# Attention and a gated feed-forward in one program: merged score visits, a planner with transfer times by kind, and 136 small matmuls on constants at the start

## The chip, the cores and the metric

The kernel runs on one core of one Trainium2 chip. The metric is the device time of one execution in microseconds. Engines: TensorE (PE; its weight loads are PEld), VectorE (DVE), ScalarE (ACT), GpSimd (POOL), and SyncE (SP), which here issues every DMA.

## The reference

Causal attention over 4 batches, 12 heads, 448 tokens and 64 numbers per head, then a gated feed-forward on 1792 tokens:

```python
scores = scale * np.matmul(q, k.transpose(0, 1, 3, 2))
scores = np.where(mask, -1000000000.0, scores)
attn = np.exp(scores - np.max(scores, axis=-1, keepdims=True))
attn = attn / (np.sum(attn, axis=-1, keepdims=True) + 1e-09)
x = np.matmul(attn, v)          # then heads side by side: 1792 x 768
a = x @ w1
b = x @ w2
h = a * b @ w3
return h @ w_out
...
```

w1 and w2 are 768x1024, w3 1024x1024, w_out 1024x768. The weights arrive as 64-bit floats, q, k and v as 32-bit floats.

## The kernel before

**The work.** Weights are decoded to f32 on chip: two ScalarE passes (lines 681, 683), a shift on VectorE (685) and an integer add on VectorE or GpSimd (688). Since h is only multiplied by w3 and then w_out, the product W3W_out is made once (`w34`: transposes of w3 on line 768, f32 products on 780). For every batch, six pairs of heads give values x (`pair`), then the gate products x w1 and x w2 (`gate`, lines 904 to 906), then the projection by W3W_out (`project`, 964 to 966). f16 operands are split into a high and a low half, so each product is three matmuls.

**A pair of heads.** q and k are turned on TensorE (batches 0 and 1, line 492) or by DMA (batches 2 and 3). Scores (line 575) use half of the array's rows per head for three blocks of query rows (128x128, 128x256, 128x384 of scores) and a quarter of the array for the last 64 rows (64x448). VectorE adds the mask and takes the maximum (592), ScalarE the exponential (596). The result is scaled and split (621 to 628), transposed by DMA, and multiplied with the values (648, 653), where half of the array's columns serve each head. So TensorE's array has four shapes: whole, row halves, quarters, column halves; the planner calls them `mode`.

**What sets the order.** Every step is put into `Program` with a due time, its possible engines with a cost for each, and what it reads and writes. `order()` then runs a list schedule: at each time the ready step of the lowest due time goes on the engine that is free first. This plans PSUM banks, engines and the DMA queue, and the instructions are emitted in that order; at run time each engine goes through its list in order and waits where it must. Due times come from the numbers in `PLAN`. Before, a transfer costs its size over one rate (181 or 330 GB/s) and the queue is free again after a fixed time. A planned change of mode costs `SWITCH`.

**The places that the change touches:** `PLAN` (27), `add` (64), `order` (90), the constants (292), `dma` (440), `scores` (565), its calls in `pair` (635), `raw` (695), `take_w3` (745).

Of the kernel before, what the change touches and what calls it, by code (L numbers as in the profile page):

```python
# [26 lines left out]
PLAN = dict(nc=10, wstep=3.6064, soft=-6.8718, w0=50.8305, w34=0.7706, ab=1.9504, out=0.6632, gap=-1.6322, lat=44.2335, begin=-91.0074, wlead=70.5419, urgent=-469.9817, flex=370.3401, sc=-41.0893, vo=-494.4237, av=-194.2706, x=-353.7633, qlead=-514.025, rlead=417.269, v0=250.3178, v1=137.6978, gram=2, nf=3, h0=0, hv=1, ns=7, wo0=372.2276, wo1=301.1492, wom=91.9573, w3a=767.9653, w3l=46.2422, wd=-104.1576, wh=-132.8946, wl=1.1959, fin=-10.7242, ev=483.517, po=[7.835, -22.3194, -46.2642, -45.7187, -46.1544, -168.5123, 44.732, 118.2718, -2.1469, -154.505, -36.8352, 4.8443, 45.9944, -62.3407, -59.3789, -141.4965, -13.9926, -146.366, -84.3586, -180.0751, 32.2385, 37.7583, 62.9194, 45.468], wo=[94.042, -8.263, -88.9315, -217.7217, 115.6771, 99.8526, 211.7957, -24.8481], w3=[-158.8005, -50.8167, -61.9442, -32.663, -51.9857, -143.9432, 16.037, 208.3012], tw=[-214.4914, 58.2404, 21.4694, -22.4979, -112.6908, -172.2348, -114.743, -134.9378, -53.1451, -19.9257, -4.9187, -20.2346, -61.9799, -199.5703, -107.2525, -134.2498], slack=0.1918, pflex=136.6935, fq=2, hlead=80.6809, stick=24.2514, wfrom=6)  # L27
# [10 lines left out]
WINDOW, PHASE = 3.413, 1.65  # L38

# [11 lines left out]
class Program:  # L51
# [3 lines left out]
    def __init__(self):  # L55
        self.ops, self.writer, self.readers, self.modes = [], {}, {}, {}
        self.port, self.lock = set(), set()
        self.banks, self.leased, self.first = {}, [], {}
# [5 lines left out]
    def add(self, due, how, reads=(), writes=(), stage=None, mode=None, port=False, lock=False):  # L64
# [18 lines left out]
        if mode:  # L83
            self.modes[i] = mode
        if port:
            self.port.add(i)
# [11 lines left out]
    def order(self):  # L98
# [11 lines left out]
        ran = [None] * n  # L110
        dma_free, last_mode, lock_end, port_end = 0.0, None, 0.0, 0.0
# [28 lines left out]
        while len(result) < n:  # L140
# [41 lines left out]
            if e == SP:  # L182
                move, turn = cost
                dma_free = max(dma_free, t + (1.275 if turn else 1.1)) + move
                free[e] = max(t + 0.65, dma_free - 0.93) if turn else t + 0.475
                end = dma_free + 0.91
            else:
# [9 lines left out]
                if e == PE and cost:  # L197
                    mode = self.modes.get(i)
                    if mode != last_mode:
                        cost += SWITCH  # L200
                        last_mode = mode
                    end = matmul(t, cost)
# [40 lines left out]
def tile_causal_attention_moe(ctx: ExitStack, tc: tile.TileContext, q, k, v, w1, w2, w3, wo, out):  # L243
    nc = tc.nc
# [47 lines left out]
    nc.vector.memset(ones, 1.0)  # L292
    mask = cst.tile([P, 3 * P], BF16, name="mask")
# [146 lines left out]
    def dma(dst, src, due, reads, writes, size, turn=False, rate=330e3):  # L440
        kw = {"transpose": True} if turn else {}
        prog.add(due, (SP, (size / (181e3 if turn else rate), turn),
# [15 lines left out]
    def take_v(b, half, due):  # L458
# [7 lines left out]
        for c in range(4):  # L466
            rows = min(P, S - c * P)
            dma(t[0:rows, c], v[b, heads, c * P : c * P + rows].rearrange("h p d -> p h d"), due - 6, (), [vk[c]],
                NP * rows * D * 4, rate=181e3)
# [11 lines left out]
    def turned_whole(p, b, hs, T, qk, qkk, qt, qtk):  # L481

        for i, src in ((1, k), (0, q)):
            dma(qk[0:QP, i], src[b, hs].rearrange("h (p r) d -> p r h d", r=4),
                T - PLAN["qlead"], (), [qkk + (i,)], 2 * S * D * 4, rate=181e3)
# [15 lines left out]
    def halved(p, b, hs, T, qk, qkk, qt, qtk):  # L501
# [4 lines left out]
        for i, src in ((1, k), (0, q)):  # L506
            raw_k = [qkk + (i, n) for n in range(3)]
            for h in range(2):
                dma(qk[:, i, 0:3, h], src[b, hs.start + h, 0 : 3 * P].rearrange("(c p) d -> p c d", p=P), T - PLAN["qlead"],
                    [], [raw_k[h]], 3 * P * D * 4, rate=181e3)  # L510
            dma(qk[0:D, i, 3], src[b, hs, 3 * P : S].rearrange("h p d -> p h d"), T - PLAN["qlead"],
                [], [raw_k[2]], 2 * D * D * 4, rate=181e3)
# [23 lines left out]
    def pair(p):  # L536
# [28 lines left out]
        def scores(us, due):  # L565
            i, c, w, lo = place(us[0])
            n = min(P, S - c * P)
            banks = [prog.lease("sc") for _ in us]
            m = mask_t if i == 2 else mask[:, (2 - c) * P :]

            def products(qs, ks, start, stop):
                for j in range(2):
                    rows = slice(j * D, (j + 1) * D)
                    ps = banks[j if i < 2 else 0][0]
                    nc.tensor.matmul(ps[rows if i == 2 else slice(0, P), :w], qs[rows, c * P : c * P + n], ks[rows, 0:w],  # L575
                                     start=start, stop=stop)

            def both():
                if not halves:
                    products(qt[:, 0], qt[:, 1], True, True)  # L580
                    return
                q16 = qt.rearrange("p i f -> p (i f)").bitcast(F16).rearrange("p (i t f) -> p i t f", i=2, t=2)
                for m_, (a, b_) in enumerate(((0, 0), (0, 1), (1, 0))):
                    products(q16[:, 0, a], q16[:, 1, b_], m_ == 0, m_ == 2)

            outs = [heads[place(u)[0]] for u in us]
            prog.add(due, (PE, (3 if halves else 4) * t_mm(w) + 0.02, both), [qtk + (1,), qtk + (0,)],
                     [key for _, key in banks] + [tk + (c,) for _, tk in outs] + ([tk for _, tk in outs] if p < 2 else []),
                     mode="quad" if i == 2 else "row")
            for u, (ps, key), (t32, tk) in zip(us, banks, outs):  # L590
                o = t32[:, lo : lo + w]
                prog.add(due + 0.4, (DVE, t_dve(w) + 0.07, lambda o=o, ps=ps, u=u: nc.vector.tensor_tensor_reduce(  # L592
# [472 lines left out]
```

## Time and profile before

| | |
|---|---|
| median of 3 runs | 555.8 us (554.55 to 556.99) |
| profiled execution | 555.84 us |
| span of the profile | 554.0 us |
| TensorE busy | 537.5 us, 97% of the span |
| VectorE busy | 384.4 us, 69% |
| ScalarE busy | 323.9 us, 58% |
| GpSimd busy | 156.1 us, 28% |
| moved by DMA | 84.60 MB, mean 153 GB/s |

Busy is the time in which at least one instruction of the engine was running. Matmuls overlap one another, so a row's duration is longer than the distance to the next row's start; the distance is what one of them costs TensorE. An f32 product of line 780 shows as two records.

### The profile page before, as it was taken

What the parts mean: (1) busy time and instruction counts of PE and PEld (TensorE: products, weight loads), DVE (VectorE), ACT (ScalarE), POOL (GpSimd) and SP (SyncE); (2) the same over time, 40 slices, a digit from 0 to 9 for tenths busy, and PEclk for the clock granted to TensorE, in tenths of its full rate; (3) what the DMA queues carried; (4) which work ended last, traced back from release to release, by engine and by line L of the source; (5) the groups of instructions that cost most, each with busy time, mean ns of one, the idle gap of its engine ahead of it and who ended that gap; (6) DMA issues with size and microseconds to landing.
All of it is one profiled execution on the core that took longest, in us unless ns stands there. A gap on an engine that the chain in (4) does not pass through costs nothing.

```text
span 554.0 us, 10756 instructions
## 1 busy us (share of the span) xinstructions
PE 537.5 (97%) x3872; PEld 300.5 (54%) x3872; DVE 384.4 (69%) x1057; ACT 323.9 (58%) x774; POOL 156.1 (28%) x118
## 2 busy tenths in 40 slices
PE   2999999999999999999999999999999999999996
PEld 1565565555554555555445555655555555555564
DVE  5536999998999899984998768398986760322100
ACT  6757888798698978654664646265762551111111
POOL 4000465554566424430334203231421110000000
PEclk9999999999999999999999999999999999999999
DMA  8998599989989648998777958979899235000011
GB/s 324 289 298 233 118 217 206 229 215 240 184 216 239 153 97 151 180 178 167 107 155 142 166 128 167 185 164 159 142 142 143 61 84 115 0 2 1 14 58 43
DMA packets 224950, 84.60 MB, mean 153 GB/s; under 512 B 205952, under 2 KB 221824, under 8 KB 224896
## 3 DMA queue, kind: packets, MB, share of 16 engines
q1 hardware_dynamic: 224896, 83.91, 72.1%
q8 instruction: 30, 0.49, 0.4%
q14 instruction: 24, 0.20, 0.1%
HBM read 43.78 MB, written 5.51 MB: 89 GB/s over the span
## 4 chain that ended last, share of the span: by engine, by line
PE 82%; DVE 9%; ACT 3%; DMA 3%; issue 1%; POOL 1%; POOLq 0%; ACTq 0%
PE sc L575 8%; PE mm L780 8%; PE mm L904 7%; PE mm L905 7%; PE mm L906 7%; PE mm L964 5%; PE mm L966 4%; PE mm L965 4%; PE tr L904 4%; PE av L653 4%; PE tr L905 4%; PE tr L906 4%; PE sc L780 2%; PE tr L964 2%; PE tr L966 2%; PE tr L965 2%
## 5 line engine op out<-in xcount | busy, mean ns | idle before, releaser
L906 PE MATMUL mm<-xt,w 128*128 128x448 f16 x258 | 90.9, 352 | 1.3 <-DVE w L727 1.3
L904 PE MATMUL mm<-xt,w 128*128 128x448 f16 x258 | 91.1, 353 | 0.0
L905 PE MATMUL mm<-xt,w 128*128 128x448 f16 x258 | 90.9, 352 | 0.0
L596 ACT ACTIVATE p<-p,mx 128x384 f32<-128x384 f32 (+2 forms) x144 | 71.5, 497 | 28.7 <-DVE mx L592 28.6
L780 PE MATMUL mm<-wof,w3t 128*128 128x384 f32 x192 | 71.4, 505 | 2.5 <-POOL wof L688 2.5
L628 DVE SCALAR_TENSOR_TENSOR ph<-p,rc,ph 128x384 f16<-128x384 f32 (+2 forms) x144 | 68.6, 528 | 1.4 <-ACT ph L623 0.9
L625 POOL TENSOR_SCALAR ph<-p,rc 128x128 f16<-128x128 f32 (+2 forms) x40 | 43.1, 1086 | 69.8 <-DVE rc L606 39.5
L575 PE MATMUL sc<-qkt 64*128 64x384 f16 (+7 forms) x480 | 58.9, 356 | 0.2 <-DMA qkt<-da 0.2
L906 PEld LDWEIGHTS <-w 128*128 128x128 f16 x384 | 37.5, 98 | 37.1 <-DVE w L727 2.2
L904 PEld LDWEIGHTS <-w 128*128 128x128 f16 x384 | 37.5, 98 | 36.0 <-issue 3.5
L905 PEld LDWEIGHTS <-w 128*128 128x128 f16 x384 | 37.5, 98 | 29.7 <-issue 0.2
L964 PE MATMUL mm<-w34h,arena 128*128 128x384 f16 x152 | 49.7, 327 | 0.0
L966 PE MATMUL mm<-w34h,arena 128*128 128x384 f16 x152 | 49.5, 326 | 0.0
L965 PE MATMUL mm<-w34l,arena 128*128 128x384 f16 x152 | 49.5, 326 | 0.0
L780 PEld LDWEIGHTS mm<-wof,w3t 128*128 128x128 f32 x192 | 34.2, 193 | 24.3 <-issue 4.1
L904 PE MATMUL tr<-xt,w 128*128 128x448 f16 x126 | 44.5, 353 | 0.0
L905 PE MATMUL tr<-xt,w 128*128 128x448 f16 x126 | 44.4, 352 | 0.0
L906 PE MATMUL tr<-xt,w 128*128 128x448 f16 x126 | 44.4, 352 | 0.0
L592 DVE CUSTOM_DVE_ANT_0 p<-sc,mask,qiv 128x384 f32<-128x384 f32 (+2 forms) x72 | 31.4, 478 | 18.0 <-PE sc L575 17.8
L930 ACT CAST arena<-g 128x448 f16<-128x448 f32 x22 | 12.4, 563 | 49.2 <-DVE g L925 49.2
L623 ACT ACTIVATE ph<-p,rc 128x384 f16<-128x384 f32 (+2 forms) x64 | 29.1, 504 | 9.5 <-issue 5.7
L685 DVE TENSOR_SCALAR da<-da 128x768 int32<-128x768 int32 (+1 forms) x38 | 24.2, 639 | 14.9 <-ACT da L681 14.7
(182 smaller groups left out, 1028.8 us busy)
## 6 DMA issues: line engine op xcount, KB each, us to landing
arena<-in_moe_w_dram SPq DMA_DIRECT2D x11, 768.0 KB, 5.7
vr<-in_v_dram SPq DMA_DIRECT2D x24, 192.0 KB, 3.9
out_dram<-osb SPq DMA_DIRECT2D x24, 192.0 KB, 2.2
arena<-in_moe_w_dram SPq DMA_DIRECT2D x8, 512.0 KB, 5.1
xt<-in_moe_w_dram SPq DMA_DIRECT2D x5, 768.0 KB, 8.0
qkr<-in_k_dram SPq DMA_DIRECT2D x12, 224.0 KB, 6.3
qkr<-in_q_dram SPq DMA_DIRECT2D x12, 224.0 KB, 6.9
arena<-in_moe_w_out_dram SPq DMA_DIRECT2D x3, 768.0 KB, 9.3
```

The costliest lines, as they stand in the source:

```text
L575: nc.tensor.matmul(ps[rows if i == 2 else slice(0, P), :w], qs[rows, c * P : c * P + n], ks[rows, 0:w], start=start, stop=stop)
L592: prog.add(due + 0.4, (DVE, t_dve(w) + 0.07, lambda o=o, ps=ps, u=u: nc.vector.tensor_tensor_reduce(out=o, in0=ps[:, :w], in1=m, scale=iv, ...
L596: prog.add(due + 0.9, (ACT, t_act(w, pointers=1, acc=True), lambda o=o, u=u: nc.scalar.activation(out=o, in_=o, func=AF.Exp, scale=-1.0, b ...
L625: (POOL, 1.1 * (t_pool(w) + 0.35e-3 * w + 0.16), lambda src=src, r=r, h=h: nc.gpsimd.tensor_scalar(out=h, in0=src, scalar1=r, scalar2=None ...
L628: prog.add(due + 0.4, (DVE, t_dve(w) + 0.06, lambda src=src, r=r, h=h, l=l: nc.vector.scalar_tensor_tensor(out=l, in0=src, scalar=r, in1=h ...
L780: prog.add(due, (PE, 4 * t_mm(NH), lambda: nc.tensor.matmul(ps[:, :NH], w3t[slot(m)][:, g], wof[:, g, ns], start=g == 0, stop=g == KF - 1) ...
L904: nc.tensor.matmul(ps[:, :S], w[:, 0, d], xh, start=d == 0, stop=False)
L905: nc.tensor.matmul(ps[:, :S], w[:, 0, d], xl, start=False, stop=False)
L906: nc.tensor.matmul(ps[:, :S], w[:, 1, d], xh, start=False, stop=d == KD - 1)
L964: nc.tensor.matmul(t, gh[:, fc, cs], w34h[:, fc, ns], start=fc == 0, stop=False)
L965: nc.tensor.matmul(t, gh[:, fc, cs], w34l[:, fc, ns], start=False, stop=False)
L966: nc.tensor.matmul(t, gl[:, fc, cs], w34h[:, fc, ns], start=False, stop=fc == KF - 1)
```

## The change

The scores of the second and the first block of a pair go into one step: their results lie side by side in the same PSUM bank (columns 0 to 255 and 256 to 383), TensorE makes them in one visit, and a pair leases five score banks instead of seven; the quarters may use bank `tr` too. The planner gets the transfer's rate by kind (164 to 430 GB/s), a count of its packets with a limit on those under way, engines that begin at different times, and a due time for each half of a w3 row; all numbers of `PLAN` are new. 34 steps without inputs, of four 128-column products of a constant each (136 matmuls), stand last in line for TensorE, so `order()` puts them where nothing else is ready.

```diff
-PLAN = dict(nc=10, wstep=3.6064, soft=-6.8718, ...
+PLAN = dict(nc=10, wstep=6.9304, soft=-564.0239, ... join=0, nwarm=34, w3h=[-138.4231, ...
+BEGIN = {PE: 1.3, ACT: 2.1, DVE: 0.85, POOL: 1.3, SP: 0.5}
+RING = 2150
...
-        free = {e: 0.0 for e in (PE, ACT, DVE, POOL, SP)}
+        free = dict(BEGIN)
...
-                move, turn = cost
-                dma_free = max(dma_free, t + (1.275 if turn else 1.1)) + move
-                free[e] = max(t + 0.65, dma_free - 0.93) if turn else t + 0.475
+                move, turn, count = cost
+                begun = max(dma_free, t + (1.07 if turn else 1.22))
+                dma_free = begun + move
                 end = dma_free + 0.91
+                if turn:
+                    free[e] = max(t + 0.65, dma_free - 0.6 - 0.5 * move)
+                else:
+                    free[e] = t + (0.6 if count > 800 else 0.43)
+                    total = count
+                    for a, b, m in reversed(moves):
+                        if b <= free[e]:
+                            break
+                        if total + m > RING:
+                            free[e] = max(free[e], b - (b - a) * (RING - total) / m)
+                            break
+                        total += m
+                    moves.append((begun, dma_free, count))
...
+    def idle_work():
+        ps, key = prog.lease("tr", "mm", "sc")
+
+        def products():
+            for i in range(4):
+                nc.tensor.matmul(ps[:, i * P : (i + 1) * P], ones, ones, start=True, stop=True)
+
+        prog.add(1e6, (PE, 4 * t_mm(P), products), (), [key])
+
+    for _ in range(PLAN["nwarm"]):
+        idle_work()
...
-        def scores(us, due):
-            i, c, w, lo = place(us[0])
-            n = min(P, S - c * P)
-            banks = [prog.lease("sc") for _ in us]
+        def scores(groups, due):
+
+            blocks = []
+            for us in groups:
+                i, c, w, lo = place(us[0])
+                if c == 0:
+                    shared, at = blocks[-1][1], blocks[-1][2] + blocks[-1][4][2]
+                else:
+                    shared, at = [prog.lease("sc") if i < 2 else prog.lease("sc", "tr") for _ in us], 0
...
-        for n, us in enumerate(((2, 5), (1, 4), (6,), (0, 3))):
-            scores(us, T + PLAN["sc"] + 0.6 * n)
+        for n, groups in enumerate(([[(2, 5)], [(1, 4), (0, 3)], [(6,)]], [[(2, 5), (6,)], [(1, 4), (0, 3)]])[PLAN["join"]]):
+            scores(groups, T + PLAN["sc"] + 0.6 * n)
...
             for h in range(2):
+                d = due + h + (PLAN["w3h"][m] if h else 0.0)
                 ns = slice(h * n, (h + 1) * n)
-                t, tk = raw(words(w3[m * P : (m + 1) * P, ns]), n, due + h - PLAN["rlead"])
-                decode(t, tk, n, due + h, w3p[:, ns], [("w3s", h)])
+                t, tk = raw(words(w3[m * P : (m + 1) * P, ns]), n, d - PLAN["rlead"])
+                decode(t, tk, n, d, w3p[:, ns], [("w3s", h)])
```

**The order that comes of it.** First TensorE at its start. Before, transposes of w3 (`tr`) and the first products of w_out with a transposed w3 (`mm`, `sc`) follow one another:

```order
L768 MATMUL tr_70<-ident,arena 128x128 x8
L780 MATMUL mm_64<-wof,w3t_122 128x384
L780 MATMUL mm_65<-wof,w3t_122 128x384
L768 MATMUL tr_70<-ident,arena 128x128 x4
L780 MATMUL sc_66<-wof,w3t_123 128x384
```

Now (136 small matmuls on `ones`, of which the first and the last of each group are shown):

```order
L318 LDWEIGHTS ones
L318 MATMUL mm_64<-ones 128x128
...
L814 MATMUL tr_70<-ident,arena 128x128 x4
L318 LDWEIGHTS ones
L318 MATMUL sc_67<-ones 128x128
...
L826 MATMUL mm_64<-wof,w3t_122 128x384
L826 MATMUL mm_65<-wof,w3t_122 128x384
L826 MATMUL mm_64<-wof,w3t_122 128x384
L826 MATMUL mm_65<-wof,w3t_122 128x384
L814 MATMUL tr_70<-ident,arena 128x128 x4
L523 MATMUL sc_66<-ident,qkr_82 128x112 x4
```

Before the first product now stand 72 small matmuls, four transposes, 52 small ones, four transposes and 12 small ones; then four products of the first two blocks of w_out, and the turns of k and q earlier than before.

SyncE's first transfers, before (in_moe_w_dram is w3 here; the w_out block, `xt`, is third):

```order
L443 DMA arena<-in_moe_w_dram 128x1024 x2
L443 DMA xt_101<-in_moe_w_out_dram 128x1536
L443 DMA w34h<-in_moe_w_dram 128x1024
L443 DMA w34l<-in_moe_w_dram 128x1024
L443 DMA w34h<-in_moe_w_out_dram 128x1536
```

and now:

```order
L474 DMA w34l<-in_moe_w_dram 128x1024
L474 DMA arena<-in_moe_w_dram 128x1024
L474 DMA xt_101<-in_moe_w_out_dram 128x1536
L474 DMA w34h<-in_moe_w_out_dram 128x1536
L474 DMA w34h<-in_moe_w_dram 128x1024
L474 DMA w34l<-in_moe_w_dram 128x1024
L474 DMA qkr_82<-in_k_dram 112x8x64
L474 DMA qkr_82<-in_q_dram 112x8x64
```

(one more w3 piece into `arena` stands ahead of both lists' second row). Two blocks of w_out come after three pieces of w3, and k and q of the first pair right behind seven transfers.

Third, the score products of the first pair on TensorE (`qkt_84`). Before:

```order
L575 MATMUL sc_69<-qkt_84 128x384
L575 MATMUL sc_66<-qkt_84 128x384
L407 LDWEIGHTS ones
L407 MATMUL sc_67<-w34m_126,ones 128x1
L780 MATMUL sc_68<-wof,w3t_124 128x384
L780 MATMUL mm_64<-wof,w3t_122 128x384 x2
L575 MATMUL sc_69<-qkt_84 128x256
L575 MATMUL sc_66<-qkt_84 128x256
L780 MATMUL mm_64<-wof,w3t_122 128x384
L768 MATMUL tr_70<-ident,arena 128x128 x4
```

Now:

```order
L826 MATMUL sc_66<-wof,w3t_124 128x384
L826 MATMUL av_63<-wof,w3t_124 128x384
L613 MATMUL sc_67<-qkt_84 128x256
L613 MATMUL sc_68<-qkt_84 128x256
L613 MATMUL sc_67<-qkt_84 128x128
L613 MATMUL sc_68<-qkt_84 128x128
L523 MATMUL sc_69<-ident,qkr_82 128x112 x4
```

The 256-wide and the 128-wide block are one visit, with no whole-array work between them. Over the whole program TensorE's list changes the shape of the array 168 times before and 130 times now; f32 products of line 780 (now 826) stand right behind scores, values or a small bf16 product 21 times before and 16 times now.

## Rows read from the trace of the kernel before

**Rows 1.** Busy time by stretch; columns: length, PE, PEld, DVE, ACT, POOL, clock, DMA share, GB/s.

```profile
0.00:50.00 50.00, 39.45 (x144) 23.44 (x144) 23.91 (x42) 33.15 (x51) 6.86 (x15) 1.00 1.07 303
50.00:150.00 100.00, 98.97 (x646) 56.76 (x648) 94.01 (x249) 82.26 (x198) 52.17 (x32) 1.00 0.93 195
150.00:250.00 100.00, 99.56 (x776) 55.64 (x771) 94.77 (x267) 79.92 (x187) 45.79 (x30) 1.00 0.86 176
250.00:350.00 100.00, 99.78 (x851) 54.06 (x850) 78.42 (x236) 57.66 (x160) 26.73 (x23) 1.00 0.79 146
350.00:450.00 100.00, 100.00 (x845) 54.66 (x845) 73.38 (x218) 51.73 (x145) 22.83 (x18) 1.00 0.78 142
```

**Rows 2.** Timeline of TensorE's start: start us, us, engine, instruction, [idle before <-releaser].

```profile
6.67 1.08 PE L768 MATMUL tr<-ident,arena 128*128 128x128 f32 x4 [6.67 <-DVE arena L688]
12.01 2.93 PE L780 MATMUL mm<-wof,w3t 128*128 128x384 f32 x4 [2.46 <-POOL wof L688]
14.73 1.06 PE L768 MATMUL tr<-ident,arena 128*128 128x128 f32 x4
16.96 1.46 PE L780 MATMUL sc<-wof,w3t 128*128 128x384 f32 x4
```

**Rows 3.** Busy time by stretch, the first 20 us.

```profile
0.00:10.00 10.00, 2.20 (x8) 1.43 (x8) 4.02 (x12) 5.96 (x9) 2.45 (x12) 1.00 0.79 286
10.00:20.00 10.00, 7.31 (x22) 4.39 (x23) 8.05 (x11) 8.64 (x14) 3.13 (x2) 1.00 1.09 371
```

**Rows 4.** Timeline, the last matmul.

```profile
549.46 0.33 PE L966 MATMUL mm<-w34h,arena 128*128 128x384 f16 x1
```

**Rows 5.** Timeline of TensorE, from gate products to scores.

```profile
255.03 0.35 PE L905 MATMUL tr<-xt,w 128*128 128x448 f16 x1
255.21 0.35 PE L906 MATMUL tr<-xt,w 128*128 128x448 f16 x1
255.50 0.66 PE L575 MATMUL sc<-qkt 64*128 64x384 f16 x6
```

**Rows 6.** Timeline of TensorE: f32 products in a run, and after scores.

```profile
25.09 0.81 PE L780 MATMUL sc<-wof,w3t 128*128 128x384 f32 x2
25.74 0.81 PE L780 MATMUL av<-wof,w3t 128*128 128x384 f32 x2
...
53.54 0.91 PE L780 MATMUL mm<-wof,w3t 128*128 128x384 f32 x2
54.29 0.60 PE L768 MATMUL tr<-ident,arena 128*128 128x128 f32 x4
54.72 0.49 PE L780 MATMUL mm<-wof,w3t 128*128 128x384 f32 x1
```

**Rows 7.** Timeline of TensorE: three places where it waited.

```profile
141.38 0.36 PE L906 MATMUL mm<-xt,w 128*128 128x448 f16 x1 [1.03 <-DVE w L727]
...
179.21 0.36 PE L906 MATMUL mm<-xt,w 128*128 128x448 f16 x1 [0.27 <-DVE w L727]
...
272.78 0.97 PE L575 MATMUL sc<-qkt 64*128 64x384 f16 x11 [0.22 <-DMA qkt<-da]
```

**Rows 8.** Timeline of TensorE: products with a weight load each, and what follows.

```profile
153.31 1.42 PE L855 MATMUL sc<-xt 128*128 128x128 f16 x23
154.66 0.20 PE L407 MATMUL sc<-vam,ones 128*128 128x1 bf16 x2
```

**Rows 9.** Timeline of ScalarE and VectorE: decoding one block of w_out.

```profile
8.28 0.91 ACT L681 ACTIVATE da<-xt 128x768 f32<-128x768 f32 x1
...
14.90 0.96 DVE L688 CUSTOM_DVE_ANT_0 wof<-w34h,da 128x1536 uint16<-128x1536 uint16 x1
```

**Rows 10.** Groups by form: xcount | busy us, mean ns of one | idle before.

```profile
L722 DVE TENSOR_SCALAR w<-da,w_s 128x768 f16<-128x768 f32 x4 | 3.9, 979 | 0.1
L628 DVE SCALAR_TENSOR_TENSOR ph<-p,rc,ph 128x384 f16<-128x384 f32 x48 | 31.1, 650 | 0.4 <-POOL ph L625 0.4
...
L855 PEld LDWEIGHTS <-xt 128*128 128x128 f16 x72 | 4.3, 98 | 0.7
```

More of the change, by code (lines that the diff above doesn't have):

```diff
@@ L484, in turned_whole @@
             dma(qk[0:QP, i], src[b, hs].rearrange("h (p r) d -> p r h d", r=4),
[L485 removed]
+                T - PLAN["qlead"], (), [qkk + (i,)], 2 * S * D * 4, rate=172e3, count=2 * S)
         for i in (1, 0):
@@ L574, in products @@
                     ps = banks[j if i < 2 else 0][0]
-                    nc.tensor.matmul(ps[rows if i == 2 else slice(0, P), :w], qs[rows, c * P : c * P + n], ks[rows, 0:w],
+                    nc.tensor.matmul(ps[rows if i == 2 else slice(0, P), at : at + w], qs[rows, c * P : c * P + n], ks[rows, 0:w],
                                      start=start, stop=stop)
             def both():
-                if not halves:
-                    products(qt[:, 0], qt[:, 1], True, True)
-                    return
@@ L582, in both @@
[L582 to L589, printed above, removed]
@@ L590, in scores @@
-            for u, (ps, key), (t32, tk) in zip(us, banks, outs):
-                o = t32[:, lo : lo + w]
-                prog.add(due + 0.4, (DVE, t_dve(w) + 0.07, lambda o=o, ps=ps, u=u: nc.vector.tensor_tensor_reduce(
-                    out=o, in0=ps[:, :w], in1=m, scale=iv, scalar=-NEG,
-                    op0=ALU.add, op1=ALU.min, accum_out=mx[:, u : u + 1])),
-                    [key, ivk, "mask_t" if i == 2 else "mask"], [mk + (u,), tk + (c,)] + ([tk] if p < 2 else []))
-                prog.add(due + 0.9, (ACT, t_act(w, pointers=1, acc=True), lambda o=o, u=u: nc.scalar.activation(
-                    out=o, in_=o, func=AF.Exp, scale=-1.0, bias=mx[:, u : u + 1], accum_out=sm[:, u : u + 1])),
-                    [mk + (u,)], [tk + (c,), smk + (u,)])
+                for block in blocks:
+                    if not halves:
+                        products(block, qt[:, 0], qt[:, 1], True, True)
+                        continue
+                    q16 = qt.rearrange("p i f -> p (i f)").bitcast(F16).rearrange("p (i t f) -> p i t f", i=2, t=2)
+                    for m_, (a, b_) in enumerate(((0, 0), (0, 1), (1, 0))):
+                        products(block, q16[:, 0, a], q16[:, 1, b_], m_ == 0, m_ == 2)
@@ new lines, in scores @@
+            keys = {id(l): l for b_ in blocks for _, l in b_[1]}
+            outs = [(heads[place(u)[0]][1], b_[4][1]) for b_ in blocks for u in b_[0]]
+            mode = ["quad" if b_[4][0] == 2 else "row" for b_ in blocks]
+            cost = sum((3 if halves else 4) * t_mm(b_[4][2]) + 0.02 for b_ in blocks) + SWITCH * (mode[0] != mode[-1])
+            prog.add(due, (PE, cost, both), [qtk + (1,), qtk + (0,)],
+                     list(keys.values()) + [tk + (c,) for tk, c in outs] + ([tk for tk, _ in outs] if p < 2 else []),
+                     mode=mode[0], leave=mode[-1])
@@ new lines, in scores @@
+            for us, banks, at, m, (i, c, w, lo) in blocks:
+                for u, (ps, key) in zip(us, banks):
+                    t32, tk = heads[place(u)[0]]
+                    o = t32[:, lo : lo + w]
+                    prog.add(due + 0.4, (DVE, t_dve(w) + 0.07, lambda o=o, ps=ps, u=u, at=at, w=w, m=m: nc.vector.tensor_tensor_reduce(
+                        out=o, in0=ps[:, at : at + w], in1=m, scale=iv, scalar=-NEG,
+                        op0=ALU.add, op1=ALU.min, accum_out=mx[:, u : u + 1])),
+                        [key, ivk, "mask_t" if i == 2 else "mask"], [mk + (u,), tk + (c,)] + ([tk] if p < 2 else []))
+                    prog.add(due + 0.9, (ACT, t_act(w, pointers=1, acc=True), lambda o=o, u=u: nc.scalar.activation(
+                        out=o, in_=o, func=AF.Exp, scale=-1.0, bias=mx[:, u : u + 1], accum_out=sm[:, u : u + 1])),
+                        [mk + (u,)], [tk + (c,), smk + (u,)])
```

34 lines of the change are left out of this document (21 added, 13 removed).

## The prediction

> **What bounds the kernel now.** I read the stretches first, because they show which engine is full and when. TensorE is busy 98.97 to 100.00 of every 100 us from 50 us to 450 us; only the first 50 us have a hole, 39.45 busy of 50 [rows 1]. The other engines have room over the whole span, but VectorE (DVE) is at 94.01 and 94.77 of 100 in the two stretches from 50 to 250 us [rows 1]: it is the second bound. A busy TensorE need not be a productive one, so the next view is the start of its timeline, and then the distance from one instruction's start to the next's. The profiled execution took 555.84 us with a span of 554.0; the median of the runs is 555.8, so a sum made against the one holds for the other.
>
> The start shows two losses. TensorE does nothing until 6.67 us, when the first piece of w3 is decoded, and waits 2.46 us before its first product at 12.01 [rows 2]. And it is slow: four product records (two products) take 2.93 us at 12.01 and 1.46 at 16.96 [rows 2]. The granted clock reads 1.00 in both ten-microsecond stretches [rows 3], but twice the time for the same form is the lower level, 1.2 GHz, against 2.4 later. The transposes at 14.73 are still slow, the row at 16.96 is at full pace [rows 2]: the engine had then worked for some 4.5 us since 12.01, with no hole as long as a microsecond.
>
> From 16.96 us to the last matmul, which ends at 549.8 [rows 2, 4], TensorE is a queue without holes. A row of the gate products follows its neighbour by 0.18 to 0.19 us (255.03, 255.21), but the row that changes the shape of the array (whole array to the 64-row halves of the scores) comes 0.29 later [rows 5]: a change of shape costs 0.09 to 0.10 us. A second small price: two f32 records just after scores take 0.75 us to the next start (53.54 to 54.29), two in the middle of a run 0.65 (25.09 to 25.74) [rows 6]; 0.10 per return. True waits are few: 1.03 us at 141.38 and 0.27 at 179.21 for a weight that VectorE makes, 0.22 at 272.78 for a transfer [rows 7]; 1.5 us, and the rest is smaller.
>
> **The change part by part.** *The start.* The rows after the change put 136 small matmuls ahead of the first real products: 72, four transposes, 52, four transposes, 12. Their operand is ready at about 1 us. They cost time only if they last longer than the data take. 23 products, most of 128 columns and each with its own weights, take from 153.31 to 154.66 [rows 8], 0.059 us on the mean; at half pace 0.118. If the pace doubles after 4.5 us of work, as it did between 12.01 and 16.96 [rows 2], 38 run slowly until 5.6, the other 34 of the first group until 7.6, transposes until 8.1 (0.44 for four, from 54.29 to 54.72 [rows 6]; the row reads 0.60 there and 1.06 at 14.73), 52 until 11.1, transposes until 11.6, 12 until 12.3.
>
> When are the data there? The transfers come in the new order: three w3 pieces of 0.52 MB, two w_out blocks of 0.79, two w3 pieces, k, q. 2.86 MB had moved by 10 us, then 371 GB/s went on [rows 3]. The first block (2.36 MB in all) lands at about 8.9, the second (3.15) at 10.8, the next w3 pieces at 12.2 and 13.6, k at 14.2, q at 14.8. A block needs two ScalarE passes of 0.91 and one VectorE join of 0.96 [rows 9], 2.8: ready at about 11.7 and 13.6. So the first product stands ready at 11.7 and the small matmuls let it go at 12.3; two products take 1.3, the next two start at 13.6 anyhow and end at 14.9. Transposes and k, q turns follow as their data come, to 16.8. By then real work of 16 transposes (1.75), four products (2.6) and eight turns (about 0.75) is done, 5.1 us at full pace, and by 16.96 5.25. The kernel before had by 16.96 done 16 transposes and two products, 3.05. **Gain 2.2 us**, at most 3.1 (no hole between 11.7 and 16.8), and at worst a loss (rival 2).
>
> *Fewer changes of shape.* In the order, rows of TensorE change their shape 168 times before and 130 times after: scores of two blocks share a bank and a visit, and the planner keeps a shape longer. 38 x 0.093 (0.29 less the usual distance [rows 5]) makes **3.5 us less**, since the path runs over TensorE wherever that falls; 24 of the 38 lie between the start of the second and the third batch's gate products, after 250 us, where VectorE is at 78 of 100 [rows 1]. Returns to f32 products right after other work fall from 21 to 16: 5 x 0.10, **0.5 us less**. The products themselves are the same in number and shape.
>
> *Waits.* The new plan is made with transfer times by kind instead of one rate, but the trace cannot show its waits. Bounds: none (1.5 us less) and, if each of 24 pairs met its transfer as late as the one at 272.78 did, 24 x 0.22, 5.3 us more. I take **no change**, since the order in hand was also a plan and came out with these 1.5 us in 533; that row is nearer than either end.
>
> *What hides the rest.* 136 matmuls are not on the path while data are missing; if they outlast the data, all of them are. VectorE takes work over from GpSimd: up to the last value of the second batch its order has five joins and three weight scalings more (0.96 and 0.98 us for 768 columns [rows 9, 10]; two joins have 512) and a few small ones, less five copies of attention values, about 5 us; its idle time hides them (rival 1 if not). The tail after 549.8 (4.2 us of scaling and output) [rows 4] is the same.
>
> Sum: 555.84 - 2.2 - 3.5 - 0.5 = **549.6 us**.
>
> A rule against the start's gain is the Trainium skill's, in "TensorE: Matmul & The Clock Gate", section "Back-to-back issue gap": in a stream of weight loads and matmuls one of 128 columns takes about 81 ns, not the isolated gap. The measurement here, 59 ns with the weights loaded each time [rows 8], speaks against it. By 81 ns the small matmuls would end at about 14.4 instead of 12.3, and the sum, by an estimate from that page, would be 551.6; with the loads as the limit this is the milder form of rival 2 below.
>
> **The rivals.**
>
> *1. VectorE becomes the bound (slower).* For: it idles only 11.2 us between 50 and 250 [rows 1], and up to the second batch's last value its order holds about 11 us more work than before: some 5 as above, the rest softmax work of one more pair pulled ahead (seven remainders, 0.65 for the widest common one [rows 10], and four score passes, about 6). TensorE arrives earlier by 2.2 + 0.5 + 12 x 0.093, 3.8. Against: before the first scale of a finished W3W_out row the new order has about 7 us more of this work (14 instructions at some 0.5: qk copies, score passes, decodes), in the first 50 us, where VectorE was busy 23.91 of 50 [rows 1]. That leaves 11 - 7 = 4 to find, and 11.2 - 4 - 3.8 = 3.4 us idle: enough if it can be used. If VectorE keeps all of its 11.2 idle (waits for others), the stretch is 7.8 longer than planned, 557.4; if the early part is not used either, 14.8, 564.4. I price it at 560. It decides if VectorE still idles over about 6 us there.
>
> *2. The small matmuls stay at the low pace.* Then 136 x 0.118 = 16.0, two groups of transposes at 0.87, and the first product starts at 18.9 with 0.9 of real work done, where before about 5.0 was (3.05 at 16.96): 4.1 lost, and 4.5 us more at half pace, 2.2. With the later 4.0 gained: 555.84 + 4.1 + 2.2 - 4.0 = 558.1. For: nothing shows that products on constants bring the pace up. Against: the start [rows 2], where transposes and products did. A milder form: their weight loads, 0.098 us each [rows 10], do not hide behind them and set the distance. Then the same chain ends at 16.1 (34, 52 and 12 at 0.098), 1.7 of work is done at 16.96 against 3.05, and the time is 549.6 + 2.2 + 1.35, 553.1. Against: 0.059 measured with loads [rows 8].
>
> *3. New waits for transfers.* The plan's order does not meet the transfers where it expects them, 5.3 us as bounded above, or the start is held by q: 549.6 + 3.5 to 5.3, 553 to 555. For: one queue issues all transfers in order, so one late piece holds those behind it. Against: only 0.22 us [rows 7] is such a wait now.
>
> *4. Waits go too.* All 1.5 of them, and a start without a hole (0.9): 549.6 - 2.4, 547.2. For: the planner now knows more of the transfers. Against: two of the three waits are for VectorE.
>
> **How the numbers follow.** The forecast (547.5 to 552) has 0.57, rival 1 0.11, rival 2 0.04 and its milder form 0.05 (at the border, half faster and half same), rival 3 0.15, rival 4 0.08. No change means within 0.5%, about what a measurement of this kernel can tell, 553.0 to 558.6. Faster: 0.57 + 0.08 + 0.03 = 0.68. Same: rival 3, from the border up, rival 2 and half its milder form, 0.15 + 0.04 + 0.02 = 0.21. Slower: rival 1, 0.11. The range leaves out rival 1 (0.11), rival 2 (0.04) and a part of rival 4 (0.03): 546.5 to 557.
>
> **What would show it.** Right: small matmuls at 0.12 us and then 0.06 us apart, the doubling at 5 to 6 us, first product (line 826) at 12 to 12.5 and all rows at full pace, TensorE's work level with before's 2 us earlier at 20 us; 130 changes of shape at 0.09; the last matmul at about 543.5; VectorE above 95 of 100 between 50 and 250 with TensorE still full. Wrong: TensorE idle for VectorE between 100 and 250 (rival 1), a first product after 14 us (rival 2), rows that wait for DMA on pt, qkt or qkr (rival 3). A last matmul later than 549.8 refutes the whole.

## The result and the profile after

The changed kernel takes **562.36 us** (median of 4 runs, 561.28 to 562.74) against 555.21 for the kernel before (4 runs): a ratio of 1.012, 95% interval 1.009 to 1.015. The profiled execution has 562.64 us and a span of 560.9. It is slower, where 549.6 was predicted.

Busy time by stretch of the changed kernel (columns as in [rows 1]):

```profile
0.00:50.00 50.00, 47.24 (x272) 31.79 (x272) 26.75 (x52) 34.79 (x53) 5.54 (x14) 1.00 1.03 302
50.00:150.00 100.00, 97.49 (x668) 57.96 (x668) 93.87 (x245) 83.75 (x197) 45.62 (x29) 1.00 0.96 203
150.00:250.00 100.00, 96.34 (x704) 53.90 (x702) 94.24 (x261) 77.03 (x186) 40.90 (x26) 1.00 0.74 161
250.00:350.00 100.00, 97.95 (x804) 55.14 (x806) 69.33 (x212) 51.95 (x137) 19.83 (x17) 1.00 0.71 139
350.00:450.00 100.00, 96.63 (x838) 54.66 (x834) 76.62 (x232) 57.07 (x157) 18.59 (x18) 1.00 0.78 140
```

Between 50 and 450 us TensorE is idle for 2.51 + 3.66 + 2.05 + 3.37 = 11.6 us; before it was 1.7 [rows 1]. That is the loss, and it lies in every stretch, also where VectorE is at 69 of 100. The first 50 us look fuller only because of the products on constants.

What TensorE waited for, by line (total us, times, longest):

```profile
PE av L692 <- DMA ptt<-pht: 5.7, 5, 1.6
PE sc L438 <- ACT da L425: 1.6, 3, 0.6
PE sc L523 <- DMA qkr<-in_k_dram: 1.3, 2, 0.7
PE sc L613 <- DVE mx L636: 1.2, 4, 0.5
...
PE sc L412 <- DVE mx L636: 0.9, 1, 0.9
```

The largest are values (line 692) that wait for the transposed scores `ptt`. In [rows 7] no wait was of this kind. They are half of the 11.6 us; the rest is spread over waits for `da`, `qkr`, `mx` and others. The places, in TensorE's timeline:

```profile
197.74 0.22 PE L412 MATMUL sc<-diag,ones 128*128 128x128 bf16 x1 [0.92 <-DVE mx L636]
250.53 0.57 PE L692 MATMUL av<-ptt,v 128*64 128x64 f16 x24 [1.44 <-DMA ptt<-pht]
260.38 0.57 PE L692 MATMUL av<-ptt,v 128*64 128x64 f16 x24 [0.87 <-DMA ptt<-pht]
267.40 0.16 PE L438 MATMUL sc<-qam,ones 128*128 128x2 bf16 x1 [0.65 <-ACT da L425]
352.26 0.57 PE L692 MATMUL av<-ptt,v 128*64 128x64 f16 x24 [1.53 <-DMA ptt<-pht]
371.24 0.57 PE L692 MATMUL av<-ptt,v 128*64 128x64 f16 x24 [1.56 <-DMA ptt<-pht]
...
556.30 0.33 PE L1012 MATMUL mm<-w34h,arena 128*128 128x384 f16 x1
```

The last row answers [rows 4]: the last matmul starts 6.8 us later. Of all 24 values steps I measured how long after the landing of its last transposed piece each starts. The median was 2.04 us before and is 0.82 now; one of 24 stood closer than 0.5 us before, ten do now.

SyncE's list (SPq) shows why these pieces are late:

```profile
241.50 5.55 SPq L474 DMA_TRANSPOSE pt<-ph  x2
247.15 1.26 SPq L474 DMA_TRANSPOSE ptt<-pht  x1
248.50 1.29 SPq L474 DMA_TRANSPOSE qkt<-da  x1
249.88 0.53 SPq L1028 DMA_DIRECT2D out_dram<-osb  x1
250.46 0.43 SPq L474 DMA_DIRECT2D qkr<-in_q_dram  x1
250.99 0.47 SPq L1028 DMA_DIRECT2D out_dram<-osb  x1
251.51 1.11 SPq L474 DMA_DIRECT2D qkr<-in_q_dram  x2
252.78 3.76 SPq L474 DMA_TRANSPOSE pt<-ph  x2
256.64 1.82 SPq L474 DMA_TRANSPOSE ptt<-pht  x1
258.56 2.43 SPq L474 DMA_DIRECT2D vr<-in_v_dram  x4
```

Each issue begins within 0.2 us of where the one before it ends. The `ptt` issued at 247.15 had its data at 241.58 (the end of the last VectorE row that writes `pht`) and stood 5.6 us in the list; it landed at 250.40, and values began at 250.53. Tracing the chain back from the last matmul, to the row before on the same engine where it followed without a gap and otherwise to what released it, I find before some 490 of 549 us on TensorE and 30 on SyncE's list and its transfers; it leaves TensorE behind the two waits for `w` in [rows 7], at 114 to 141 and at 165 to 180 us. Now some 280 of 556 are on TensorE and 195 on SyncE's list and its transfers. These shares shift by tens of us with how small a gap counts as none; that TensorE has far fewer of them now does not. From 226 to 265 us the chain is on SyncE and its transfers, then 2.4 us on ScalarE, and comes back to TensorE at 267.40.

The DMA engines were as busy at that time before. The same 40 us, before and then now (columns as in [rows 1]):

```profile
222.00:262.00 40.00, 40.00 (x395) 23.19 (x394) 29.91 (x90) 21.23 (x59) 10.55 (x8) 1.00 0.99 179
222.00:262.00 40.00, 36.74 (x364) 21.82 (x363) 36.16 (x106) 27.62 (x80) 15.75 (x13) 1.00 0.97 192
```

Their share is 0.99 and 0.97, yet TensorE had no idle time there before and has 3.3 us now.

The start answers [rows 2]:

```profile
5.72 1.48 PE L318 MATMUL sc<-ones 128*128 128x128 bf16 x12
7.00 0.42 PE L318 MATMUL mm<-ones 128*128 128x128 bf16 x4
...
12.97 3.11 PE L826 MATMUL mm<-wof,w3t 128*128 128x384 f32 x8 [0.42 <-DVE w3t L821]
...
17.39 0.60 PE L523 MATMUL sc<-ident,qkr 112*128 112x112 f32 x4 [0.56 <-DMA qkr<-in_k_dram]
...
19.04 2.76 PE L826 MATMUL sc<-wof,w3t 128*128 128x384 f32 x8
```

The small products are 0.107 us apart (12 in 1.28 us) up to 7.0 and 0.056 after it, so the pace doubles as forecast, though at 7.0 us and not at 5.6. But the first f32 product starts at 12.97, and k holds the list until 17.39. By 19.04 TensorE has done four of these products (eight records, 0.325 us each at full pace), four groups of transposes (0.46) and two of turns (0.38), 5.2 us of work. The kernel before had done as much by then: four groups of transposes and 3.4 us of products.

### The profile page after: what moved, and what is told of

It is laid out like the page before. It is cut to its first block, busy times and chain, and to the rows that moved or that the text cites. A ratio compares the mean times of both kernels' runs of the same rounds, so it can differ in the third digit from the quotient of the medians.

```text
span 560.9 us, 11053 instructions
## 1 busy us (share of the span) xinstructions
PE 541.8 (97%) x4008; PEld 313.4 (56%) x4008; DVE 388.0 (69%) x1064; ACT 327.5 (58%) x777; POOL 136.3 (24%) x108
## 5 line engine op out<-in xcount | busy, mean ns | idle before, releaser
L640 ACT ACTIVATE p<-p,mx 128x384 f32<-128x384 f32 (+1 forms) x144 | 71.3, 497 | 24.4 <-DVE mx L636 24.4
L672 DVE SCALAR_TENSOR_TENSOR ph<-p,rc,ph 128x384 f16<-128x384 f32 (+2 forms) x144 | 66.3, 520 | 5.0 <-ACT ph L667 4.0
L826 PE MATMUL mm<-wof,w3t 128*128 128x384 f32 x192 | 68.8, 495 | 0.4 <-DVE w3t L821 0.4
L669 POOL TENSOR_SCALAR ph<-p,rc 128x128 f16<-128x128 f32 (+2 forms) x42 | 39.6, 950 | 98.6 <-DVE rc L650 71.5
L1010 PE MATMUL mm<-w34h,arena 128*128 128x384 f16 x168 | 54.9, 327 | 0.0
L1012 PE MATMUL mm<-w34h,arena 128*128 128x384 f16 x168 | 54.8, 326 | 0.0
L1011 PE MATMUL mm<-w34l,arena 128*128 128x384 f16 x168 | 54.8, 326 | 0.0
L826 PEld LDWEIGHTS mm<-wof,w3t 128*128 128x128 f32 x192 | 34.2, 190 | 21.9 <-issue 1.8
L613 PE MATMUL sc<-qkt 64*128 64x384 f16 (+7 forms) x406 | 42.7, 339 | 1.4 <-DVE mx L636 1.2
L976 ACT CAST arena<-g 128x448 f16<-128x448 f32 x21 | 11.9, 565 | 50.9 <-DVE g L971 50.9
L729 DVE TENSOR_SCALAR da<-da 128x768 int32<-128x768 int32 (+1 forms) x38 | 21.8, 577 | 18.8 <-ACT da L725 18.8
L971 DVE SCALAR_TENSOR_TENSOR g<-mm,y,at 128x448 f32<-128x448 f32 x15 | 10.2, 681 | 34.2 <-PE mm L952 34.1
```

Source lines behind the costliest of these rows:

```text
L613: nc.tensor.matmul(ps[rows if i == 2 else slice(0, P), at : at + w], qs[rows, c * P : c * P + n], ks[rows, 0:w], start=start, stop=stop)
L640: prog.add(due + 0.9, (ACT, t_act(w, pointers=1, acc=True), lambda o=o, u=u: nc.scalar.activation(out=o, in_=o, func=AF.Exp, scale=-1.0, b ...
L669: (POOL, 1.1 * (t_pool(w) + 0.35e-3 * w + 0.16), lambda src=src, r=r, h=h: nc.gpsimd.tensor_scalar(out=h, in0=src, scalar1=r, scalar2=None ...
L672: prog.add(due + 0.4, (DVE, t_dve(w) + 0.06, lambda src=src, r=r, h=h, l=l: nc.vector.scalar_tensor_tensor(out=l, in0=src, scalar=r, in1=h ...
L826: prog.add(due, (PE, 4 * t_mm(NH), lambda: nc.tensor.matmul(ps[:, :NH], w3t[slot(m)][:, g], wof[:, g, ns], start=g == 0, stop=g == KF - 1) ...
L1010: nc.tensor.matmul(t, gh[:, fc, cs], w34h[:, fc, ns], start=fc == 0, stop=False)
```

## The experiments

Ratios are to the kernel before, measured beside each run on the same chip; the changed kernel's own is 1.012. The kernel before took 555.2 to 556.6 us beside the different runs, so a ratio tells more than a time. Every kernel keeps the planned order but for the edit shown. Theory A says that the new order leaves values no distance from their transfers and each wait is lost for good; Q, that the transfers are the limit of some stretches; V, that VectorE is; C and D concern the products on constants.

### Does a wait, taken away, stay away? (e1, e2)

```diff
 order = prog.order()
+order = pull(prog, order, {1136: 3.0, 1183: 2.5, 1791: 3.0, 1911: 3.0, ...}, last_w0)
```

`pull` puts so many us of later whole-array products, whose data are planned to be there, ahead of the step. The edit names a fifth place too, where nothing moved.

> The changed kernel, same order, but at four of the values products that waited for the transposed scores (profile rows at 250.53, 260.38, 352.26 and 371.24, idle 1.44, 0.87, 1.53 and 1.56 us, 5.40 in all) 2.3 to 3.0 us of whole-array products that stand a little later in TensorE's list are put ahead of them. Theory A (no cushion: the order puts values too near the landing of their transfers, and each such wait is lost for good): the four rows lose their wait and the last matmul comes 4.5 to 5.4 us earlier, time about 557.4. Theory B (the waits are only where lateness shows; TensorE's list is held back by VectorE anyway, so that time comes back as waits for mx or w elsewhere): the time stays within 1 us of the changed kernel, 561.5 to 562.5, with other waits grown by 4 us or more.

Measured: 563.75 us, ratio 1.013 (1.011 to 1.015). **No gain.** TensorE's waits for `da` and `ptt` in e1 (total us, times, longest):

```profile
PE sc L468 <- ACT da L455: 3.6, 4, 1.5
PE av L722 <- DMA ptt<-pht: 3.5, 3, 1.9
```

Two of the places in its timeline:

```profile
276.37 0.16 PE L468 MATMUL sc<-qam,ones 128*128 128x2 bf16 x1 [1.45 <-ACT da L455]
...
361.56 0.57 PE L722 MATMUL av<-ptt,v 128*64 128x64 f16 x24 [1.89 <-DMA ptt<-pht]
```

Waits for `ptt` fell by 2.2 us, those for `da` (the sums of squares of q and v, which wait for q and v to land) rose by 2.0. TensorE ran 1.2 us ahead of the changed kernel at 270 us and gave it back at 276; between 250 and 270 the instructions of VectorE and ScalarE started, in the median, within 0.1 us of where they did without the edit. So theory A falls in its simple form: the list that sets the pace there is not TensorE's. That it is VectorE's, as theory B has it, is not shown either: the waits that grew are those for `da`, by 2.0 us, where B gave 4 or more for `mx` or `w`.

> As the run before, and at ten other places too, where TensorE waited in the changed kernel for VectorE (mx), for ScalarE (da, w) or for k and q (qkr, qkt): 0.5 to 2.3 us of later whole-array products go ahead of the waiting step. Those waits are another 4.5 us. Theory A (each wait is lost for good, whoever it is for): 552.5 to 554. Theory B (VectorE's rate is the bound from 100 to 250 us): no better than the run before, or 1 to 2 us at most, as new waits for VectorE come where the work that was put ahead is missing.

Measured: 568.73 us, 1.021 (1.018 to 1.024): worse than e1, beyond what either theory gave.

### The products on constants (e3, e12)

```diff
+order = [x for x in order if x[1] not in idle]
```

> The changed kernel in the same order without its 136 products on constants (they compute nothing that is read). Theory C (they fill time in which no data have landed, and raise TensorE's pace before the first transposes): without them the first transposes, starting at about 7.9, run at half pace, so that the first f32 products come 0 to 1 us later, and the time is 562.4 to 564. Theory D (they delay the first transposes and products, which stand behind them in the list, and that is why the start gained nothing): the time falls by 1 to 2.5 us, to 560 to 561.4. If the start is set by k and w3 landing, both vanish: 562.0 to 562.8.

Measured: 563.45 us, 1.012 (1.009 to 1.015), as with them. They delay nothing, so D falls. The interval is some 1.7 us wide to either side, so the up to 1 us of help that C gives them is neither shown nor excluded.

e12 is the reverse:

```diff
+IDLE = {0: ("mm", 16), 1: ("mm", 3), 2: ("sc", 10)}
+if e == PE and seen in IDLE:
+    idle_products(*IDLE[seen])
```

> The kernel before, in its own order, with 116 products on constants ahead of its first transposes, between those and the next ones, and ahead of the first f32 product; all is computed. It tests the first term of the prediction by itself (the start at full pace, 2.2 us). In the changed kernel the small products went to 0.056 us apart at 7.0 us, and its start gained nothing since k and w3 landed no sooner. If the pace alone is worth it: the first f32 product still waits for its weights at 12.0, but takes 1.3 us in place of 2.6 and what follows half as long, 1.5 to 2.2 us less than before: 553 to 554. If the data's landing sets the start: within 0.5 us of before.

Measured: 557.39 us, 1.0014 (0.9999 to 1.0028): no gain. TensorE's start in e12:

```profile
12.12 1.56 PE L787 MATMUL mm<-wof,w3t 128*128 128x384 f32 x4 [1.24 <-POOL wof L695]
13.92 0.66 PE L775 MATMUL tr<-ident,arena 128*128 128x128 f32 x4 [0.24 <-POOL arena L695]
17.20 0.66 PE L775 MATMUL tr<-ident,arena 128*128 128x128 f32 x4 [2.62 <-ACT w3t L781]
...
19.45 2.68 PE L787 MATMUL mm<-wof,w3t 128*128 128x384 f32 x4
```

and a stretch of it (columns as in [rows 1]):

```profile
18.50:21.90 3.40, 3.40 (x7) 1.69 (x6) 1.85 (x5) 2.55 (x4) 0.00 (x0) 0.50 1.12 266
```

The first two f32 products take 1.56 us, where [rows 2] have 2.93. What they won is then spent waiting for ScalarE's copy at 17.20. And behind this wait of 2.62 us the granted clock falls to 0.50 (1.2 GHz): the four records at 19.45 take 2.68 us, where [rows 2] have 1.46 at 16.96. Matched instruction by instruction, TensorE is 2.4 us behind the profile of the kernel before from 20 us on. So a quicker beginning is not kept while the data come when they do. What a start at full pace throughout would be worth e12 does not show, since it had none: in nine of its twelve runs the mean granted clock is 0.993 to 0.996, as in the profiled one.

### Transfers or VectorE? (e5 to e8)

```diff
-dma(t[0:rows, c], v[b, heads, ...
+dma(t[0:rows, c, 0 : 1 if b else NP], v[b, half * NP : half * NP + (1 if b else NP), ...
-out=out[tok : tok + m, ns], in_=later["osb"][i][r : r + m]
+out=out[tok : tok + 8, ns], in_=later["osb"][i][r : r + 8]
```

> The changed kernel in the same order, but from the second batch on each v transfer brings one head of six (32 KB of 192) and each store writes 8 rows of its 128; attention values and most output rows are therefore not the reference's. Every transfer is still issued. Traced back from its last matmul, the chain of waits of the changed kernel runs over SyncE's list of transfers without a break from 222 to 267 us and again at 330 to 346; 36 transfers are issued between 222 and 262, 14 of them these. Theory Q (the transfers of these stretches are the limit, and TensorE's waits are where that shows): 3 to 6 us less than the changed kernel, 556.5 to 559.5, and waits for ptt and da mostly gone. Theory V (VectorE's list is the limit): within 1 us of the changed kernel.

> The same two shortenings in the kernel before (same outputs left out). Its chain, traced back in the same way, is TensorE from 12 to 264 us and from 273 us to the end, with one excursion over VectorE and a transfer of 8.7 us. Theories Q and V alike: TensorE is the bound here, nothing to gain but that one wait of 0.22 us: 554.5 to 555.8.

Measured: e5 555.00 us, 0.998 (0.996 to 1.000); e6 554.92 us, 0.998 (0.996 to 1.000). The edit is worth 1.4% of the time to the changed kernel and 0.2% to the one before, and **the difference between the two kernels is gone**. The gain in e5 is more than the 3 to 6 us that Q gave. Busy time by stretch in e5:

```profile
250.00:350.00 100.00, 99.43 (x831) 55.88 (x826) 70.60 (x218) 53.76 (x141) 19.91 (x19) 1.00 0.63 119
350.00:450.00 100.00, 98.46 (x847) 55.48 (x846) 77.41 (x232) 56.66 (x156) 20.73 (x20) 1.00 0.72 124
```

TensorE's waits for `ptt` in e5 (5.7 us in the changed kernel; Q had them mostly gone):

```profile
PE av L692 <- DMA ptt<-pht: 3.6, 4, 1.4
```

The row of e5's timeline that answers 267.40 in the changed kernel:

```profile
264.58 0.18 PE L438 MATMUL sc<-qam,ones 128*128 128x2 bf16 x1
```

That small product comes 2.8 us earlier and waits for nothing. Matched instruction by instruction, e5's TensorE is 2.3 us behind the changed kernel's at 100 us, level at 210, 2.8 ahead at 280, still 2.8 at 340 and 4.9 at 400: what it is ahead at the end is gained in the two stretches where the chain ran over transfers. The chain itself does not become what it was before: traced as above, some 315 of 551 us are on TensorE and 160 on SyncE's list and its transfers. Between 50 and 450 us e5's TensorE still idles 6.8 us, 5.1 more than the kernel before; that the times are equal all the same fits the 4.0 us that fewer changes of shape and f32 re-entries save.

```diff
-out=ai, in0=ai, scalar1=3, ...
+out=ai[:, :8], in0=ai[:, :8], scalar1=3, ...
```

> The changed kernel in the same order, but the shift of every weight decode on VectorE works on 8 columns of 512 or 768; the decoded weights are therefore not the reference's. It takes about 0.5 us from each of 40 steps, 20 us of VectorE's 388, most of it before 250 us. Theory V (VectorE's list, 94 of 100 busy between 50 and 250 us, is the limit): 3 to 7 us less, 555.5 to 559.5, waits for mx, da and ptt shorter. Theory Q (transfers are): within 1.5 us of the changed kernel.

> The same shortening in the kernel before (weights not decoded as the reference has them). Theory V and theory Q alike: its chain is TensorE, VectorE ended one wait of 1.03 us and one of 0.27 us there, and the start has 0.7 us of a shift on its path: 553.5 to 555.5. Were VectorE the limit of both kernels, it would fall as far as the changed one does.

Measured: e7 561.21 us, 1.009 (1.006 to 1.012); e8 555.17 us, 0.997 (0.995 to 1.000). Both kernels win about 0.3%; VectorE's 20 us do not explain the difference. V falls.

### Issue or bytes? (e9, e10)

```diff
-nc.sync.dma_start(out=out[tok : tok + m, ns], ...
+nc.scalar.dma_start(out=out[tok : tok + m, ns], ...
```

> The changed kernel in the same order, but the stores of the output (32, of which 24 are full blocks) are issued by ScalarE's queue, not SyncE's. Nothing is left out and the same bytes move. In the changed kernel a store holds SyncE's list for 0.5 to 0.6 us, and six of them stand between 228 and 262 us, where the list is never empty. Theory Q1 (SyncE's issue, one transfer after the other, is the limit of the crowded stretches): 2 to 4 us less, 558.5 to 560.5. Theory Q2 (the bytes and packets under way are the limit, however they are issued): within 1 us of the changed kernel, 561.5 to 563.

Measured: 564.06 us, 1.014 (1.012 to 1.016): no gain, Q1 falls. In the profiled execution the granted clock fell to 0.5 twice (last section), but the two runs with a mean clock of 0.998 and 1.00 took 564.00 and 563.25 us beside 556.39 for the kernel before, no gain either. The Trainium skill's "DMA: Bandwidth & Descriptors", section "Issuing engines are not separate DMA queues", says that such transfers run on the same 16 DMA engines and only the issuing engine's time is saved; by that rule nothing was to be had once the transfers themselves are the limit, and the run agrees.

> The changed kernel with the v transfers alone shortened as before (one head of six from the second batch on; attention values are not the reference's); stores are whole. Both shortenings gave 7.4 us. Theory Q2: the v transfers took 24 x 160 KB out of the way, stores 24 x 180 KB, so about half, 3 to 4.5 us: 558 to 559.5. If it is one place alone (the v transfers at 138 to 146 and 258 to 265 us, on whose scale TensorE waits at 147.25 and 267.40), 5 us or more: 557 or less.

Measured: 558.75 us, 1.005 (1.003 to 1.006): 0.74% of 556.4, 4.1 us, within what Q2 gave. So the gain is not that of the v transfers at one place; it goes about as the amount taken out of the way.

### Moving the other transfers back (e11)

```diff
+order = defer(prog, order, last_w0, 6.0, 3.0)
```

> The changed kernel, all computed, but 43 of the 200 ordinary transfers (k, q, v, weights and stores whose reader comes at least 3 us after their planned landing) go up to 6 us later in SyncE's list, behind the transposes that follow them. Theory Q: what waits is the transposes, which stood ready 2 to 5.6 us behind such transfers, so values wait less: 1 to 3 us less, 559.5 to 561.5. If the queue's whole throughput is what lacks there, the waits only change their names (da, qkr, qkt for ptt): 562 to 564.

Measured: 569.65 us, 1.023 (1.021 to 1.026): 6 us worse than the changed kernel, beyond both. Waits for `ptt` did not fall (7.4 us instead of 5.7), those for `da` rose from 1.6 to 2.4 and those for `qkt` from 0.2 to 2.3: what was put back was late in its turn, and the transposes gained nothing by it.

### What distance is worth, and whether full transfers explain e1 (e4, e13, e14)

```diff
+order = early(prog, order, 2.6, last_w0)
```

> The kernel before, in its own order, with 18 of the 24 values steps moved 0.6 to 3.1 us ahead in TensorE's list, past whole-array products that now follow them. Nothing else differs: scores apart, the old transfer times, no products on constants. In its trace a values step starts 2.0 us (median of 24) after its last transposed piece has landed, in the changed kernel 0.9. Theory A: the cushion is what is taken away, and the waits that come of it, worked out step by step from the 24 distances, are 11.6 us if none is given back: 8 to 12 us slower, 563 to 567, with waits for ptt at the values steps. Theory B (what a late transfer costs is won back by fewer waits after it): within 2 us of 555.2.

Measured: 565.91 us, 1.017 (1.014 to 1.020), 9.3 us slower, as theory A gave. Its waits for `ptt`, where the kernel before had none:

```profile
PE av L674 <- DMA ptt<-pht: 7.2, 9, 1.9
```

> The changed kernel with the shortened v transfers and stores (attention values and most output rows are not the reference's), and with 1.7 to 3.1 us of later whole-array products put ahead at five places where TensorE still waited then: values at 98.64, 248.73, 258.27 and 366.62 (idle 1.41, 0.32, 0.57, 1.29 us) and the small product at 197.87 (0.92), 4.5 us in all. Theory Q (in the changed kernel such moves gave nothing because the queue of transfers was full and TensorE only met it again at the next transfer): with the queue relieved they are worth 2.5 to 4.5 us, 550.5 to 552.5. Rival (in-order lists of all engines are tied to one another, and a wait taken away at one place returns at the next whatever the transfers do): 554.5 to 557.

Edit: `pull` as in e1, on e5. Measured: 556.07 us, 0.999 (0.997 to 1.001); e5 had 0.998. **The rival holds.** Waits that were taken away came back elsewhere:

```profile
203.52 0.57 PE L722 MATMUL av<-ptt,v 128*64 128x64 f16 x24 [1.98 <-DMA ptt<-pht]
...
371.85 0.16 PE L468 MATMUL sc<-vam,ones 128*128 128x1 bf16 x1 [1.22 <-ACT da L455]
```

> The kernel before with 18 values steps moved ahead as before (0.6 to 3.1 us, which cost 9.3 us) and the shortened v transfers and stores (outputs left out as there). Theory Q (the loss is made where late transfers meet a cushion that is too small): with transfers that land earlier most of it goes, 556 to 559.5. Rival (the values were put ahead of the landing that even an empty queue gives, so the distance alone is the loss): 562 to 565.

Edit: e4 with e5's shortenings. Measured: 565.42 us, 1.016 (1.012 to 1.019). The rival holds here too: against e6 the values moved ahead still cost 1.8%. So there are two prices. Values put closer to their landing cost nearly the whole distance in the old list (9.3 of the 11.6 us worked out), whatever else is under way (e4, e14). In the new list a large part of the waits is made by the v transfers and stores that share the queue (e5, e10).

## Why the prediction was wrong, by its own steps

**Changes of shape, -3.5: right as far as a row shows.** The trace has 38 fewer, as the order had, and one costs what it did; a whole-array product ahead of scores:

```profile
193.73 0.35 PE L952 MATMUL tr<-xt,w 128*128 128x448 f16 x1
194.01 1.35 PE L613 MATMUL sc<-qkt 64*128 64x384 f32 x8
```

0.28 us to the next start where 0.189 is usual, 0.093 more, as in [rows 5]. The saving is in the sum below; the waits outweigh it.

**f32 re-entries, -0.5:** fewer by the order; not measured by itself.

**The start, -2.2: wrong, about 0.** The step that failed is when the data are there, "k at 14.2, q at 14.8". The prediction let 371 GB/s go on from 10 us and took each piece to land when the bytes up to it had moved. The changed kernel moved less in that stretch (columns as in [rows 1]):

```profile
10.00:20.00 10.00, 8.72 (x69) 5.99 (x67) 7.54 (x12) 6.60 (x10) 0.40 (x1) 1.00 1.07 321
```

and pieces issued later shared it: the two blocks of w_out landed at 9.57 and 11.46 us instead of 8.9 and 10.8, the next w3 pieces at 14.11 and 16.05 instead of 12.2 and 13.6, k at 17.34 and q at 18.34. TensorE waited for k up to 17.39. The quick pace that the small products brought went into these waits; what it would be worth with data in time no run shows (e3, e12). On the pace the trace sides with [rows 8], 0.056 us with the weights loaded each time, against the 81 ns that the prediction weighed from the Trainium skill's "TensorE: Matmul & The Clock Gate", section "Back-to-back issue gap".

**"Waits: no change", at most +5.3: wrong, and the step that decided.** It cost 9.9 us between 50 and 450 us. The price, 24 times the 0.22 us of [rows 7], came from a kernel whose values start 2 us after their landing; that row tells how seldom a cushion of 2 us is used up, not what a transfer costs without one. Rival 3 named the mechanism (one queue, a late piece holds those behind it) and was given 0.15 and the same too small price, so the upper end of the range, 557, fell short as well.

Added up: 555.84 - 3.5 - 0.5 + 0 + 9.9, with 0.5 more idle after 450 us, is 562.2; measured 562.64. The 0.4 left I cannot assign.

**Rival 1 (VectorE becomes the bound), priced 560:** near in time, wrong in cause. VectorE has 388 us instead of 384, GpSimd 136 instead of 156, but relief of VectorE is worth the same to both kernels (e7, e8), and by the prediction's own sign VectorE still idles 11.9 us between 50 and 250, where this rival wanted under 6. **Rival 2 (small matmuls stay slow):** no; their distance halves at 7.0 us.

**Open.** The planner's transfer times, the merged scores and the table of numbers fix one order together, so no run here says which of them brought values closer to their transfers. The waits for `mx` (2.3 us, 0.2 of it below the rows shown) mostly remain in e5 (2.0); that the merged blocks hold their banks longer would fit, and was not tried. No version that computes everything beat the kernel before.

## What to carry to other kernels

Where one engine is busy 97 of 100 and its list is fixed ahead, measure how long before its use each transfer lands; a plan that spends this distance is priced by it, not by today's waits. Before moving work into a wait, trace the chain back from the end: if it runs over another engine's list, the wait may only move, as in e1 and e13. To learn whether transfers or an engine set the pace, shorten each in both kernels and compare the gains.

## What was not expected of the hardware

At the start the granted clock is recorded as 1.00 also where products run at half pace (0.107 us apart before 7.0 us, 0.056 after, above). Later, while TensorE works, it does show falls to 0.5, in three of the profiles: in e12 from 18.5 to 21.9 us (shown there), in e9 from 241.4 to 244.8 and from 371.1 to 374.5, in e11 from 272.1 to 275.5 and from 395.0 to 398.4. Each began 0.1 to 1.4 us after the end of a long wait of TensorE: 2.62 us in e12, 2.18 and 2.16 in e9, 1.91 and 2.27 in e11. One of e9's stretches (columns as in [rows 1]):

```profile
241.40:244.80 3.40, 3.40 (x21) 2.08 (x16) 1.54 (x5) 2.08 (x6) 1.56 (x1) 0.50 0.94 198
```

So each of these waits was paid for twice, with about 1.7 us more (half of such a stretch at half pace, an estimate). Waits as long did not always do it: none followed the 1.98 us of e13 or the 1.89 of e1.

The start of the kernel before is not the same in each execution. In e6, whose start is not edited, the same rows as [rows 2] read

```profile
17.38 2.77 PE L780 MATMUL sc<-wof,w3t 128*128 128x384 f32 x4
19.94 1.93 PE L780 MATMUL mm<-wof,w3t 128*128 128x384 f32 x4
21.70 1.45 PE L780 MATMUL sc<-wof,w3t 128*128 128x384 f32 x4
```

where [rows 2] have four records in 1.46 us from 16.96 on. Full pace came about 4 us later, and TensorE was 2.2 us behind from 20 us on. A single profile of the kernel before can therefore be off by 2 us at the start alone, as much as the gain that was forecast there.

In the changed kernel a transpose by DMA holds SyncE's list for a median of 1.28 us (`qkt`), 1.77 (`ptt`) or 1.85 (`pt`), most ordinary transfers for 0.4 to 0.6; two `pt` took 5.55 us at 241.50 and 3.76 at 252.78.
